# Batch 0's start in a fused linear attention and MLP kernel: k's sums as columns, k^T v in one stretch, chunk 0's denominators early

## The chip, the cores and the metric

The kernel runs on one core of a Trainium2 chip. A core has a matrix engine (TensorE, PE in the profile, with its weight loads listed as PEld), a vector engine (VectorE, DVE), an activation engine (ScalarE, ACT), a general engine (GpSimd, POOL) and a queue engine (SyncE, SP). Each runs its own stream of instructions in order; semaphores between them say when an operand is ready. PSUM is the memory that TensorE writes into, SBUF holds everything else. The metric is the device time of one execution in microseconds (us), lower is better.

## The reference

For 8 batches, 8 heads, 576 positions and head dimension 64 the reference computes a linear attention with cosine weights, and puts its output through a two-layer MLP:

```python
phi(x) = concat(relu(x) * cos_w, relu(x) * sin_w)     # 64 -> 128 features
kv  = einsum('bhsf,bhsd->bhfd', phi(k), v)            # k^T v, 128 x 64 per head
z   = sum_s phi(k)                                    # k's sums, 128 per head
num = einsum('bhsf,bhfd->bhsd', phi(q), kv)
den = einsum('bhsf,bhf->bhs', phi(q), z) + 1e-6
x   = (num / den), heads side by side                 # 4608 x 512
h   = x @ w_in                                        # 512 -> 2048
out = (h * sigmoid(1.702 * h)) @ w_out                # 2048 -> 512
```

## The kernel before

The two stages are fused batch by batch: the attention of a batch gives its x, transposed, and the MLP follows on it, while the attention of the next batch is slipped between the matmuls. The order on every engine is the order in which the program writes it (a manual schedule). Two kinds of PSUM tiles matter here: four "mm" tiles of one bank each, used in turn, and two "at" tiles of two banks each. A tile is written again only when the engine that reads it is done.

Batch 0 has nothing to be slipped between, so its attention is laid out by hand as a start, lines 386 to 436. Positions are cut in nine slices of 64 rows by 4 pairs of heads. The steps, by their helpers:

- `trig` (L142 on DVE and POOL, L140 on ACT) makes phi for one slice: two instructions, cosine and sine. k's nine slices (tile kr) come first, then q's (tile qn). k and q arrive in two transfers each from the SP queue, v for batch 0 in two transfers from POOL's queue straight into a bf16 tile vb (L132), one for heads 0 to 3 and one for heads 4 to 7. POOL's queue then brings the MLP's weights and batch 1's k, q and v.
- `idle(n)` (L348) issues n warm-up matmuls of 512 columns on a zero tile, whose result nobody reads. They keep TensorE at work; the first twelve run before any data is there.
- `ksum(j)` (L217) adds k slice j to k's sums: the weights are a 128x2 selector of the two heads of a pair, the moving operand is the slice with its 512 columns, and the result is a tile of 2 rows by 512. After the ninth slice DVE copies it to SBUF as bf16 (tile zr, L402), and `ksum_turn` (L223, L224) turns it with four small transposes and copies it into column 64 of the tile kvs.
- `qturn_pe(c)` (L171) transposes two slices of q into an mm tile, and `qevac(c)` copies them to qT, on DVE (L181) or ACT (L179). There are five turns; the last has one slice.
- `kv_mm` (L207) computes k^T v for two pairs of heads, 36 matmuls, and `kv_evac` (L212) copies the result on DVE into columns 0 to 63 of kvs. The two halves use the two at tiles.
- `num_mm(c)` (L232) multiplies chunk c of 128 positions of q with kvs for all 8 heads: 64 columns of numerators and, from column 64, the denominator. It needs an at tile. `num_div(c)` does three instructions on DVE: add 1e-6 (den, L240), reciprocal (inv, L242), multiply (xn, L244).
- `xturn_mm(c)` (L262) transposes xn into the free part of the same at tile, and `xturn_evac` (L269) copies it on ACT into x. Only then is the at tile free for the chunk after next.
- `start_block` (L357 on) runs chunks 0 to 4 between the first MLP matmuls: `mm1_part` (L285) for groups 0 to 3 in pieces of 128 columns, then the four gelus on ACT (L290), then group 4 (the fifth of sixteen, counted from zero) with 512 columns, `mm1(b, 4)`, and after it the transposes of chunk 4. Groups 0 to 3 hold all four mm tiles, so group 4 starts when the first gelu has read its own. `start_block` is called for batch 0 and, with its first turns already done, for batch 1.

The order of the start before, on TensorE: sums of slices 0, 1, 2, 3, 6, 4, 7, 5, a warm-up matmul, the sum of slice 8, a warm-up, q's turn 0, two warm-ups, turns 1 and 2, the turning of the sums, first half of k^T v, turn 3, second half of k^T v, turn 4, numerators of chunks 0 and 1, four warm-ups, then `start_block`.

Of the kernel before, what the change touches and what calls it, by code (L numbers as in the profile page):

```python
# [9 lines left out]
F32 = mybir.dt.float32  # L10
BF16 = mybir.dt.bfloat16
AF = mybir.ActivationFunctionType
MUL = mybir.AluOpType.mult
ADD = mybir.AluOpType.add
# [5 lines left out]
def kernel(  # L20
# [9 lines left out]
    nc = tc.nc  # L30
    B, H, S, D = q.shape
# [4 lines left out]
    NS = S // 64  # L36
    MT = 512
    NI = H // 2
# [6 lines left out]
    small = ctx.enter_context(tc.tile_pool(name="small", bufs=3))  # L45
    pmm = ctx.enter_context(tc.tile_pool(name="pmm", bufs=4, space=PSUM))
# [24 lines left out]
    ident = const.tile([128, 128], BF16)  # L71
# [13 lines left out]
    sel = const.tile([128, 2], BF16)  # L85
# [9 lines left out]
    kr = one.tile([128, NS, NI, 128], BF16, name="kr")  # L95
# [4 lines left out]
    qT = one.tile([128, H, 640], BF16, name="qT")  # L100
# [34 lines left out]
    def trig(dst, src, j, act=False, eng=nc.vector):  # L135
        i = src[:, :, ts(j, 64)]
        for cs, w in enumerate((cosw, sinw)):
            o = dst[:, j, :, ts(cs, 64)]
            if act:
                nc.scalar.activation(o, i, AF.Relu, scale=w[:, j:j + 1])  # L140
            else:
                eng.tensor_scalar(o, i, 0.0, w[:, j:j + 1], op0=MAX, op1=MUL)  # L142
# [24 lines left out]
    def qturn_pe(c, home=None):  # L167
        tp = pmm.tile([128, 2, NI, 128], BF16, name="mm") if home is None else home
        for j in range(2 * c, min(2 * c + 2, NS)):
            for i in range(NI):  # L170
                nc.tensor.transpose(tp[:, j % 2, i], qn0[:, j, i, :], ident)  # L171
        tps[c] = tp

    def qevac(c, act=False):
        n = min(2 * c + 2, NS) - 2 * c
        o = qT[:, :, ds(c * 128, n * 64)].rearrange("f h (j p) -> f j h p", j=n)
        i = tps.pop(c)[:, 0:n].rearrange("f j i (hh p) -> f j (i hh) p", hh=2)
        if act:
            nc.scalar.activation(o, i, AF.Copy)  # L179
        else:  # L180
            nc.vector.tensor_copy(o, i)  # L181
# [10 lines left out]
    st = {}  # L192

    def kv_open(i0=0, i1=NI):
        t = pat.tile([128, 2, 512], F32, name="at")
        for i in range(i0, i1):
            st["kv", i] = t[:, :, ds((i - i0) * 65, 65)]
        st["ps", i0] = t[:, :, 0:(i1 - i0) * 65]
        if i0 == 0:
            st["kvs"] = small.tile([128, 2, NI, VW], BF16, name="kvs", bufs=2)  # L200

    def kv_mm(i0, i1, rhs, col, n):
        for i in range(i0, i1):
            for j in range(NS):
                for hh in range(2):
                    r = slice(hh * 64, hh * 64 + 64)
                    nc.tensor.matmul(st["kv", i][:, hh, ds(col, n)], kr[r, j, i, :], rhs(r, i, j),  # L207
                                     start=(j == 0), stop=(j == NS - 1))

    def kv_evac(i0, i1, n=65):  # L210
        o = st["kvs"][:, :, i0:i1, 0:n]
        nc.vector.tensor_copy(o, st["ps", i0].rearrange("p hh (i e) -> p hh i e", e=65)[:, :, :, 0:n])  # L212

    def ksum(j):
        if j == 0:
            st["z"] = pmm.tile([128, 512], F32, name="mm")
        nc.tensor.matmul(st["z"][0:2], sel, kr[:, j].rearrange("p i f -> p (i f)"),  # L217
                         start=(j == 0), stop=(j == NS - 1))

    def ksum_turn():  # L220
        zt = pmm.tile([128, NI, 2], BF16, name="mm")
        for i in range(NI):
            nc.tensor.transpose(zt[:, i], st["zr"][:, ts(i, 128)], ident[0:2, 0:2])  # L223
        nc.vector.tensor_copy(st["kvs"][:, :, :, 64], zt.rearrange("f i hh -> f hh i"))  # L224

    nums = {}

    def num_mm(c):
        ps = pat.tile([128, 2, 512], F32, name="at")
        for h in range(H):  # L230
            i, hh = divmod(h, 2)
            nc.tensor.matmul(ps[:, h // 4, ds((h % 4) * 65, 65)], qT[:, h, ts(c, 128)],  # L232
                             st["kvs"][:, hh, i, 0:65], start=True, stop=True)
        nums[c] = [ps]

    def num_div(c):
        ps = nums[c][0]
        pv = ps[:, :, 0:260].rearrange("p a (h e) -> p a h e", h=4)
        den = small.tile([128, 2, 4], F32, name="den")
        nc.vector.tensor_scalar(den, pv[:, :, :, 64], 1e-6, None, op0=ADD)  # L240
        inv = small.tile([128, 2, 4], F32, name="inv")
        nc.vector.reciprocal(inv, den)  # L242
        xn = small.tile([128, 2, 4, 64], BF16, name="xn", bufs=4)
        nc.vector.tensor_tensor(xn, pv[:, :, :, 0:64],  # L244
                                inv.unsqueeze(3).to_broadcast([128, 2, 4, 64]), op=MUL)
        nums[c].append(xn)
# [7 lines left out]
    def x_open(b):  # L254
        x[b] = xpool.tile([128, KC, S], BF16, name="xT")

    def xturn_mm(c):
        ps, xn = nums[c]
        xv = xn.rearrange("p a h e -> p (a h e)")
        for kc in range(KC):  # L260
            o = ps[:, kc // 2, ds(264 + (kc % 2) * 64, 64)].bitcast(BF16)
            nc.tensor.transpose(o, xv[:, ts(kc, 128)], ident)  # L262

    def xturn_evac(b, c):
        ps = nums.pop(c)[0]
        n = 128 if c < 4 else 64
        i = ps[:, :, 264:392].bitcast(BF16).rearrange("p a (k t) -> p a k t", k=2)[:, :, :, 0:n]
        o = x[b][:, :, c * 128:c * 128 + n].rearrange("p (a k) t -> p a k t", a=2)
        nc.scalar.activation(o, i, AF.Copy)  # L269
# [11 lines left out]
    def mm1_part(b, fc, t0, t1):  # L281
        if t0 == 0:
            hp[fc] = pmm.tile([128, MT], F32, name="mm")
        for kc in range(KC):
            nc.tensor.matmul(hp[fc][:, t0:t1], w_in_of(kc, fc), x[b][:, kc, t0:t1],  # L285
                             start=(kc == 0), stop=(kc == KC - 1))

    def gelu(fc):
        g = gpool.tile([128, MT], BF16, name="g")
        nc.scalar.activation(g, hp.pop(fc), AF.Gelu_apprx_sigmoid)  # L290
        gT[fc] = g

    def mm1(b, fc):
        mm1_part(b, fc, 0, MT)
        gelu(fc)
# [48 lines left out]
    def idle(n, w=None):  # L344
        if w is None:
            w = pmm.tile([128, 512], F32, name="mm")
        for _ in range(n):
            nc.tensor.matmul(w, warm[:, 0:128], warm, start=True, stop=True)  # L348
        return w
# [7 lines left out]
    def start_block(b, opened=False):  # L357

        if not opened:
            xturn_mm(0)  # L360
            xturn_evac(b, 0)
            num_mm(2)
            num_div(2)
            xturn_mm(1)
            xturn_evac(b, 1)
        for c in range(4):
            for fc in range(4):
                mm1_part(b, fc, c * 128, c * 128 + 128)
            if c == 0:
                num_mm(3)  # L370
                num_div(3)
                xturn_mm(2)
                xturn_evac(b, 2)
            if c == 1:
                num_mm(4)
                num_div(4)
                xturn_mm(3)
                xturn_evac(b, 3)
        for fc in range(4):
            gelu(fc)  # L380
        mm1(b, 4)
        xturn_mm(4)
        xturn_evac(b, 4)


    w = idle(12)
# [5 lines left out]
        trig(kr, kf, j)  # L392
    kv_open(0, 2)
    kv_open(2, 4)
    for j in (0, 1, 2, 3, 6, 4, 7, 5):
        ksum(j)
    idle(1, w)
    ksum(8)
    for j in (0, 1):
        trig(qn0, qf0, j)  # L400
    st["zr"] = small.tile([2, 512], BF16, name="zr", bufs=1)
    nc.vector.tensor_copy(st["zr"], st["z"][0:2])  # L402
    idle(1, w)
    qturn_pe(0)
    for j in (2, 3):
# [10 lines left out]
    for j in (6, 7):  # L416
        trig(qn0, qf0, j, act=True)
    qevac(0)
    ksum_turn()
    qevac(2, act=True)  # L420
    kv_mm(0, 2, vb_rhs, 0, 64)
    qevac(1)
    kv_evac(0, 2, 64)
    qturn_pe(3)
    qevac(3, act=True)
    kv_mm(2, 4, vb_rhs, 0, 64)
    kv_evac(2, 4, 64)
    qturn_pe(4)
    qevac(4, act=True)
    num_mm(0)  # L430
    num_div(0)
    num_mm(1)
    num_div(1)
    idle(4)
    x_open(0)
    start_block(0)


# [61 lines left out]
    num_div(2)  # L500
    mm2(0, 3, 12, 16)
    start_block(1, opened=True)


# [78 lines left out]
```

## Time and profile before

| What | Value |
|---|---|
| Median of 3 runs | 294.69 us (294.63 to 295.33) |
| Profiled execution, its own time | 294.68 us |
| Span of the profile | 293.0 us |
| TensorE matmul busy | 287.1 us (98%) |
| TensorE weight load busy | 159.3 us (54%) |
| VectorE busy | 126.5 us (43%) |
| ScalarE busy | 131.1 us (45%) |
| GpSimd busy | 38.2 us (13%) |
| Granted TensorE clock, mean | 0.999 |

The span runs from the first to the last recorded instruction; the time of the execution has 1.7 us around it. Busy shares are averages over the whole run. The page's chain that ended last follows the work back from the last instruction, each step to what released it; by engine it is 95% PE. Matmuls are pipelined: one is listed with its latency, so the spacing of starts, not the listed duration, is what a row of them costs.

### The profile page before, as it was taken

What the parts mean: (1) busy time and instruction counts of PE and PEld (TensorE: products, weight loads), DVE (VectorE), ACT (ScalarE), POOL (GpSimd) and SP (SyncE); (2) the same over time, 40 slices, a digit from 0 to 9 for tenths busy, and PEclk for the clock granted to TensorE, in tenths of its full rate; (3) what the DMA queues carried; (4) which work ended last, traced back from release to release, by engine and by line L of the source; (5) the groups of instructions that cost most, each with busy time, mean ns of one, the idle gap of its engine ahead of it and who ended that gap; (6) DMA issues with size and microseconds to landing.
All of it is one profiled execution on the core that took longest, in us unless ns stands there. A gap on an engine that the chain in (4) does not pass through costs nothing.

```text
span 293.0 us, 5983 instructions
## 1 busy us (share of the span) xinstructions
PE 287.1 (98%) x2433; PEld 159.3 (54%) x2433; DVE 126.5 (43%) x364; ACT 131.1 (45%) x230; POOL 38.2 (13%) x70
## 2 busy tenths in 40 slices
PE   8989999999999999999999999999999999999995
PEld 2675656857455555455545554555455545565444
DVE  4864524692263826482558156715662420000000
ACT  7947752674114631463136412641265116773111
POOL 6760031500123001100110011001100010000000
PEclk9999999999999999999999999999999999999999
DMA  7999999585268965798469946986697440000322
GB/s 250 241 220 283 376 218 355 156 161 163 56 129 288 254 185 144 239 274 216 130 206 282 250 103 191 349 191 135 154 373 93 73 117 36 3 0 6 85 91 72
DMA packets 67227, 52.36 MB, mean 179 GB/s; under 512 B 47392, under 2 KB 57376, under 8 KB 67200
## 3 DMA queue, kind: packets, MB, share of 16 engines
q1 hardware_dynamic: 59824, 32.52, 45.1%
q0 software_dynamic: 7376, 19.47, 23.4%
q8 instruction: 19, 0.31, 0.4%
q14 instruction: 8, 0.07, 0.1%
HBM read 36.70 MB, written 9.44 MB: 157 GB/s over the span
## 4 chain that ended last, share of the span: by engine, by line
PE 95%; DMA 2%; DVE 1%; ACT 0%; issue 0%; SPq 0%; ACTq 0%
PE mm L335 43%; PE mm L285 38%; PE mm L303 4%; PE at L207 3%; PE at L232 3%; DMA kf<-in_k_dram 2%; PE mm L312 1%; PE at L262 1%; PE mm L171 1%; PE at L171 1%; DVE kr L142 1%; PE mm L217 0%; PE mm L348 0%; DVE xn L244 0%; ACT xT L269 0%
## 5 line engine op out<-in xcount | busy, mean ns | idle before, releaser
L335 PE MATMUL mm<-w_out_sb,g 128*128 128x512 bf16 (+1 forms) x528 | 117.7, 373 | 0.0
L285 PE MATMUL mm<-xT,w_in 128*128 128x512 bf16 (+1 forms) x608 | 113.5, 345 | 0.0
L290 ACT ACTIVATE g<-mm 128x512 bf16<-128x512 f32 x128 | 75.6, 598 | 32.0 <-PE mm L285 31.9
L285 PEld LDWEIGHTS <-w_in 128*128 128x128 bf16 x608 | 61.9, 114 | 49.0
L335 PEld LDWEIGHTS <-g 128*128 128x128 bf16 x528 | 48.7, 98 | 49.5
L339 ACT ACTIVATE ysb<-mm 128x512 f32<-128x512 f32 (+1 forms) x37 | 21.7, 586 | 111.4 <-PE mm L335 111.4
L342 POOL DMA_DIRECT2D out_dram<-ysb x38 | 20.6, 546 | 177.4 <-ACT ysb L339 177.2
L142 DVE TENSOR_SCALAR kr<-kf,cosw 128x256 bf16<-128x256 f32 x68 | 23.7, 349 | 29.0 <-DMA kf<-in_k_dram 29.0
L244 DVE TENSOR_TENSOR xn<-at,inv 128x512 bf16<-128x512 f32 x40 | 27.6, 691 | 1.4
L142 DVE TENSOR_SCALAR kr<-kf,sinw 128x256 bf16<-128x256 f32 x68 | 23.8, 350 | 0.0
L240 DVE TENSOR_SCALAR den<-at 128x8 f32<-128x8 f32 x40 | 6.6, 166 | 37.3 <-PE at L232 37.3
L232 PEld LDWEIGHTS <-qT 128*128 128x128 bf16 x320 | 14.6, 97 | 8.3 <-issue 1.0
L212 DVE CAST kvs<-at 128x520 bf16<-128x520 f32 (+1 forms) x9 | 5.8, 639 | 30.6 <-PE at L207 30.6
L232 PE MATMUL at<-kvs,qT 128*128 128x65 bf16 x320 | 16.1, 193 | 0.8 <-ACT xT L269 0.7
L155 DVE TENSOR_SCALAR qn<-qf,sinw 128x512 bf16<-128x512 f32 (+1 forms) x30 | 14.3, 477 | 0.0
L155 DVE TENSOR_SCALAR qn<-qf,cosw 128x512 bf16<-128x512 f32 (+1 forms) x30 | 14.3, 477 | 0.0
L303 PE MATMUL mm<-xt,w_in 128*128 128x384 bf16 x64 | 10.6, 326 | 0.0
L335 PE MATMUL mm<-w_out_sb,gl_t 128*128 128x512 bf16 x48 | 10.5, 379 | 0.0
L207 PEld LDWEIGHTS <-kr 64*128 64x128 bf16 x576 | 9.2, 94 | 2.3 <-issue 2.0
L303 PEld LDWEIGHTS <-w_in 128*128 128x128 bf16 x64 | 7.2, 113 | 3.3
L304 ACT ACTIVATE gl_t<-mm 128x384 bf16<-128x384 f32 x16 | 7.8, 490 | 2.4 <-PE mm L303 2.4
L163 DVE CAST vt<-vf 128x2304 bf16<-128x2304 f32 (+1 forms) x7 | 8.9, 1265 | 0.0
(68 smaller groups left out, 125.4 us busy)
## 6 DMA issues: line engine op xcount, KB each, us to landing
kf<-in_k_dram SPq DMA_DIRECT2D x5, 1152.0 KB, 6.7
vf<-in_v_dram SPq DMA_DIRECT2D x5, 1152.0 KB, 9.8
qf<-in_q_dram SPq DMA_DIRECT2D x5, 1024.0 KB, 6.0
out_dram<-ysb POOLq DMA_DIRECT2D x20, 256.0 KB, 2.8
kf<-in_k_dram POOLq DMA_DIRECT2D x2, 1152.0 KB, 10.3
vf<-in_v_dram POOLq DMA_DIRECT2D x2, 1152.0 KB, 14.0
out_dram<-ysb POOLq DMA_DIRECT2D x18, 128.0 KB, 2.9
w_in<-in_moe_w_in_dram POOLq DMA_DIRECT2D x4, 512.0 KB, 8.8
```

What stands on the lines that cost most here:

```text
L142: eng.tensor_scalar(o, i, 0.0, w[:, j:j + 1], op0=MAX, op1=MUL)
L155: nc.vector.tensor_scalar(o, i, 0.0, sc, op0=MAX, op1=MUL)
L163: nc.vector.tensor_copy(o, i)
L207: nc.tensor.matmul(st["kv", i][:, hh, ds(col, n)], kr[r, j, i, :], rhs(r, i, j), start=(j == 0), stop=(j == NS - 1))
L232: nc.tensor.matmul(ps[:, h // 4, ds((h % 4) * 65, 65)], qT[:, h, ts(c, 128)], st["kvs"][:, hh, i, 0:65], start=True, stop=True)
L244: nc.vector.tensor_tensor(xn, pv[:, :, :, 0:64], inv.unsqueeze(3).to_broadcast([128, 2, 4, 64]), op=MUL)
L285: nc.tensor.matmul(hp[fc][:, t0:t1], w_in_of(kc, fc), x[b][:, kc, t0:t1], start=(kc == 0), stop=(kc == KC - 1))
L290: nc.scalar.activation(g, hp.pop(fc), AF.Gelu_apprx_sigmoid)
L303: nc.tensor.matmul(hps, w_in_of(kc, fc), xt[:, kc, :], start=(kc == 0), stop=(kc == KC - 1))
L335: nc.tensor.matmul(yp[t, c0][:, c0:c1], w, w_out_sb[:, fc, c0:c1], start=(fc == 0), stop=(fc == FC - 1))
L339: nc.scalar.activation(ysb[:, c0:c1], yp[t, c0][:, c0:c1], AF.Identity)
L342: eng.dma_start(out=dst[:, c0:c1], in_=ysb[p0:p0 + n, c0:c1])
```

## The change

Seven edits in batch 0's start, and one in `start_block`, which batch 1 uses too:

1. `ksum(j)` takes the slice itself as weights, four times 128x128, and the selector's 2 columns as the moving operand. The sums then come out as columns, 128 rows by 4 pairs by 2 heads, in one bank: 36 matmuls of 2 columns in place of 9 of 512.
2. One copy on DVE (`ksum_evac`) brings them straight into column 64 of kvs, ahead of q's slices 4 and 5 on DVE. The tile zr, its copy and the four small transposes are gone.
3. One warm-up matmul goes ahead of each of the sums of slices 3, 6, 4, 7 and 5, five more than before.
4. `den_early(0)`: after the first half of k^T v, eight matmuls of one column (column 64 of kvs alone) give chunk 0's denominators in an mm tile; DVE adds 1e-6 and takes the reciprocal ahead of both copies of k^T v. `num_div(0)` then only multiplies.
5. The second half of k^T v and its copy move ahead of q's turn 3, the fourth turn.
6. The copy of q's turn 1 on DVE takes the place of the sums' copy, right behind that of turn 0.
7. q's turn 4 moves behind the numerators of chunks 0 and 1, its copy from ACT to DVE, behind `num_div(1)`; two warm-up matmuls follow instead of four.
8. In `start_block` the transposes of chunk 4 move ahead of `mm1(b, 4)`. Their copy on ACT stays where it was, behind group 4's gelu.

```diff
     def ksum(j):
         if j == 0:
-            st["z"] = pmm.tile([128, 512], F32, name="mm")
-        nc.tensor.matmul(st["z"][0:2], sel, kr[:, j].rearrange("p i f -> p (i f)"),
-                         start=(j == 0), stop=(j == NS - 1))
-
-    def ksum_turn():
-        zt = pmm.tile([128, NI, 2], BF16, name="mm")
+            st["z"] = pmm.tile([128, NI, 2], F32, name="mm")
         for i in range(NI):
-            nc.tensor.transpose(zt[:, i], st["zr"][:, ts(i, 128)], ident[0:2, 0:2])
-        nc.vector.tensor_copy(st["kvs"][:, :, :, 64], zt.rearrange("f i hh -> f hh i"))
+            nc.tensor.matmul(st["z"][:, i], kr[:, j, i, :], sel, start=(j == 0 and i == 0),
+                             stop=(j == NS - 1 and i == NI - 1))
+
+    def ksum_evac():
+        nc.vector.tensor_copy(st["kvs"][:, :, :, 64], st["z"].rearrange("f i hh -> f hh i"))
...
+    def inv_of(d):
+        den = small.tile([128, 2, 4], F32, name="den")
+        nc.vector.tensor_scalar(den, d, 1e-6, None, op0=ADD)
+        inv = small.tile([128, 2, 4], F32, name="inv")
+        nc.vector.reciprocal(inv, den)
+        return inv
+
+    def den_early(c):
+        d = pmm.tile([128, 2, 4], F32, name="mm")
+        for h in range(H):
+            nc.tensor.matmul(d[:, h // 4, h % 4:h % 4 + 1], qT[:, h, ts(c, 128)],
+                             st["kvs"][:, h % 2, h // 2, 64:65], start=True, stop=True)
+        return inv_of(d)
+
+    def num_div(c, inv=None):
         ps = nums[c][0]
         pv = ps[:, :, 0:260].rearrange("p a (h e) -> p a h e", h=4)
-        den = small.tile([128, 2, 4], F32, name="den")
-        nc.vector.tensor_scalar(den, pv[:, :, :, 64], 1e-6, None, op0=ADD)
-        inv = small.tile([128, 2, 4], F32, name="inv")
-        nc.vector.reciprocal(inv, den)
+        if inv is None:
+            inv = inv_of(pv[:, :, :, 64])
...
         for fc in range(4):
             gelu(fc)
+        xturn_mm(4)
         mm1(b, 4)
-        xturn_mm(4)
         xturn_evac(b, 4)
...
-    for j in (0, 1, 2, 3, 6, 4, 7, 5):
+    for j in (0, 1, 2):
+        ksum(j)
+    for j in (3, 6, 4, 7, 5):
+        idle(1, w)
         ksum(j)
     idle(1, w)
     ksum(8)
     for j in (0, 1):
         trig(qn0, qf0, j)
-    st["zr"] = small.tile([2, 512], BF16, name="zr", bufs=1)
-    nc.vector.tensor_copy(st["zr"], st["z"][0:2])
+    ksum_evac()
     idle(1, w)
     qturn_pe(0)
...
     qevac(0)
-    ksum_turn()
+    qevac(1)
     qevac(2, act=True)
     kv_mm(0, 2, vb_rhs, 0, 64)
-    qevac(1)
+    inv0 = den_early(0)
     kv_evac(0, 2, 64)
+    kv_mm(2, 4, vb_rhs, 0, 64)
+    kv_evac(2, 4, 64)
     qturn_pe(3)
     qevac(3, act=True)
-    kv_mm(2, 4, vb_rhs, 0, 64)
-    kv_evac(2, 4, 64)
-    qturn_pe(4)
-    qevac(4, act=True)
     num_mm(0)
-    num_div(0)
+    num_div(0, inv0)
     num_mm(1)
     num_div(1)
-    idle(4)
+    qturn_pe(4)
+    qevac(4)
+    idle(2)
     x_open(0)
     start_block(0)
```

More of the change, by code (lines that the diff above doesn't have):

```diff
@@ L234, in num_mm @@
         nums[c] = [ps]
-    def num_div(c):
+    def inv_of(d):
[11 more added lines that the diff above has]
+    def num_div(c, inv=None):
         ps = nums[c][0]
         pv = ps[:, :, 0:260].rearrange("p a (h e) -> p a h e", h=4)
-        den = small.tile([128, 2, 4], F32, name="den")
-        nc.vector.tensor_scalar(den, pv[:, :, :, 64], 1e-6, None, op0=ADD)
-        inv = small.tile([128, 2, 4], F32, name="inv")
-        nc.vector.reciprocal(inv, den)
+        if inv is None:
+            inv = inv_of(pv[:, :, :, 64])
         xn = small.tile([128, 2, 4, 64], BF16, name="xn", bufs=4)
```

## The prediction

> **What bounds the kernel now.** I read the busy time by stretches first, then the chain of work that ended last, then the timeline of the first 17 us. Of the stretches two rows matter (columns: busy time of PE, PEld, DVE, ACT and POOL with their instruction counts, then the granted clock, the DMA share and GB/s):
>
> ```profile
> 9.00:12.40 3.40, 3.40 (x70) 2.52 (x70) 3.28 (x10) 3.40 (x9) 2.57 (x2) 1.00 1.21 206
> ...
> 23.10:293.00 269.90, 266.51 (x2165) 146.27 (x2162) 112.05 (x318) 114.57 (x199) 23.76 (x42) 1.00 0.66 173
> ```
>
> From 23.1 us to the end PE is busy for 266.51 of 269.90 us at clock 1.00. Nothing that the change touches is there, apart from one order in batch 1, so an edit in batch 0's start is worth exactly as much as it brings forward the moment at which this dense stretch begins. That moment comes from the chain (start, length, what; a PE piece runs from the end of the instruction before it to the end of its own last one):
>
> ```profile
> 7.84 0.89 PE mm L217 x3
> ...
> 9.69 0.45 PE mm L171 x8
> 10.14 0.43 PE mm L348 x2
> 10.57 1.02 PE mm L171 x16
> 11.59 0.18 PE mm L223 x4
> 11.77 0.64 PE at L207 x36
> 12.41 0.55 PE mm L171 x8
> 12.96 0.66 PE at L207 x36
> ...
> 13.64 0.44 DVE kvs L212
> ...
> 14.12 0.29 PE at L232 x4
> ...
> 14.44 0.18 DVE den L240
> ...
> 14.64 0.21 DVE inv L242
> ...
> 14.87 0.70 DVE xn L244
> ...
> 15.62 0.41 PE at L262 x4
> ...
> 16.06 0.61 ACT xT L269
> ...
> 16.71 0.40 PE at L232 x8
> ...
> 18.22 0.24 PE at L232 x8
> ...
> 20.09 1.79 PE mm L285 x32
> ...
> 21.89 1.02 PE mm L285 x4
> 22.92 0.22 PE at L262 x4
> 23.14 9.50 PE mm L285 x44
> ...
> 39.95 0.89 PE at L171 x16
> ...
> 50.96 0.86 PE mm L335 x4
> ...
> 57.91 1.02 PE mm L285 x4
> ```
>
> The chain is TensorE alone from 7.84 to 13.6, then a relay: the copy of the second half of k^T v on DVE (13.64), chunk 0's numerators (14.12), its three divide steps on DVE (14.44, 14.64, 14.87), its transposes (15.62), their copy on ACT (16.06), and chunk 2's numerators (16.71), which need that copy to be done because it frees their PSUM tile. After them PE hardly waits. The transfers of batch 1 come early enough to leave the dense stretch alone: the latest that PE needs soon is q, whose first DVE use is the row below, while its transposes run only at the 39.95 piece above, some 6 us later.
>
> ```profile
> 33.73 0.35 DVE L142 TENSOR_SCALAR qn<-qf,cosw 128x256 bf16<-128x256 f32 x1 [2.83 <-DMA qf<-in_q_dram]
> ```
>
> **The change, step by step.** The timeline of before around the start (start, duration, engine, line):
>
> ```profile
> 1.25 4.91 PE L348 MATMUL mm<-warm 128*128 128x512 bf16 x12 [1.25 <-DVE warm L76]
> ...
> 8.29 0.49 ACT L140 ACTIVATE kr<-kf,sinw 128x256 bf16<-128x256 f32 x1
> ...
> 9.02 0.34 DVE L142 TENSOR_SCALAR qn<-qf,sinw 128x256 bf16<-128x256 f32 x1
> ...
> 9.40 0.68 DVE L402 CAST zr<-mm 2x512 bf16<-2x512 f32 x1
> ...
> 9.82 2.33 POOL L142 TENSOR_SCALAR qn<-qf,cosw 128x256 bf16<-128x256 f32 x1 [2.14 <-DMA qf<-in_q_dram]
> 9.88 0.49 ACT L140 ACTIVATE qn<-qf,sinw 128x256 bf16<-128x256 f32 x1
> ...
> 10.01 0.33 DVE L142 TENSOR_SCALAR qn<-qf,cosw 128x256 bf16<-128x256 f32 x1
> ...
> 10.80 0.34 DVE L142 TENSOR_SCALAR qn<-qf,sinw 128x256 bf16<-128x256 f32 x1
> 11.06 0.67 DVE L181 COPY qT<-mm 128x1024 bf16<-128x1024 bf16 x1
> ...
> 11.80 0.19 DVE L224 COPY kvs<-mm 128x8 bf16<-128x8 bf16 x1
> ...
> 12.15 1.13 POOL L142 TENSOR_SCALAR qn<-qf,sinw 128x256 bf16<-128x256 f32 x1
> ```
>
> The second half of v has these rows (two transfers, issued at 4.5 and 5.4):
>
> ```profile
> L132 POOL DMA_DIRECT2D vb<-in_v_dram x2: 756/835/914, 4.5 to 5.4; - x2
> ...
> DMA to landing us min/median/max: 6.2/6.5/6.8
> ```
>
> *k's sums.* Nine matmuls of 512 columns become 36 of two columns, each with its own load of 128x128 weights, and five more warm-up matmuls go between them. No row shows that form. The nearest is the four little transposes at 11.59: 0.18 for four, 0.045 each; the upper bound is a real transpose, 0.45 for eight (9.69), 0.056 each; the lower bound is a chunk's numerators, 0.24 for eight (18.22), 0.03 each with as large a load. So one k slice costs 0.18 (0.12 to 0.22), plus 0.22 for a warm-up matmul (0.43 for two, 10.14). I cost all of it at nothing up to the last slice: the slices wait for DVE and ACT, and the last one comes from ACT at 8.29 + 0.49 = 8.78. Then 0.18, a warm-up of 0.22, and q's first turn can start at about 9.2. It cannot finish before DVE's q slice 1 (9.02 + 0.34 = 9.36), four transposes and a latency of 0.2 later, so it ends near 9.8, against 10.14. If the slices cost double, this end stays, since DVE's slice covers 0.2 of it.
>
> *zr goes.* The sums were copied as 2x512 by DVE in 0.68 (9.40). The new copy is 128x8, as the one at 11.80: 0.19. It ends at about 9.5, and DVE's q slices 4 and 5 follow, 1.13 for the four (10.01 to 11.14). They also need q's second transfer, which had landed by 9.82, POOL's start on it. I take 9.7; bounds 9.5 (DVE free) and 9.82. They end at 10.83 (10.63 to 10.95) in place of 11.14.
>
> *q's turns.* Two warm-ups after 9.8 give 10.23; turn 1 needs ACT's slice 3 (9.88 + 0.49 = 10.37) and ends at 10.8; turn 2 needs the slices of 10.83, then four transposes and the latency, 0.44: it ends at 11.27, against 11.59. Four transposes of the sums (0.18) go.
>
> *k^T v and the early denominators.* The first half, 0.64, ends at 11.95. Then eight one-column matmuls for chunk 0's denominators: 0.36 at 0.045 each (0.24 to 0.45), done at 12.3. They need the first copy of qT, which on DVE moves up with the slices to about 10.75, plus 0.67: 11.42. The second half of k^T v would be next at 12.15, but it needs v's second transfer: 5.4 + 6.8 = 12.2. In before it had 0.7 us to spare there (12.96); now it is the gate. With 0.66 of work it ends near 12.95, against 13.62. So the denominators' matmuls are hidden behind v, up to 0.05.
>
> *DVE.* Denominator and reciprocal (0.18 and 0.21) are queued ahead of both copies of k^T v and wait for PE at 12.3: they end at 12.72. The two copies, 0.41 each, follow: 13.1 and, behind PE's 12.95 as well, 13.45. Before: 13.64 + 0.44 = 14.08. If the denominators came 0.3 late, the second copy would too: the new wait lies just beside the path. q's fourth turn (0.55) now runs under these copies.
>
> *Chunk 0.* Its last four numerators run from 13.5 to 13.8 (0.29; before 14.12 to 14.41). The multiply needs no denominator and no reciprocal between (0.18 + 0.21 and two handovers, 14.44 to 14.87 in the chain), so it runs from 13.82 to 14.52 instead of 14.87 to 15.57: 1.05 earlier. On PE stand meanwhile chunk 1's numerators (0.24), q's last turn (0.22; POOL's slice is done by 12.15 + 1.13 = 13.28) and two warm-ups instead of four (0.43), to about 14.5: a tie with the multiply. Transposes 0.41 and copy 0.61 with their handovers bring chunk 2's numerators to 15.63, against 16.71. **First term: 1.08 us.** q's last copy moves from ACT to DVE, behind chunk 1's multiply and ahead of chunk 2's denominators; that copy is half of 0.67, and DVE is idle there by this reckoning (multiply over at 15.5, next numerators not before 15.9), so it costs nothing; were DVE full, chunk 2 would be late by 0.35. POOL's and SP's queues keep their order and every DMA its place.
>
> *Last turns of x ahead of group 5.* After the last piece of 128-column matmuls (20.09 + 1.79 = 21.88) group 5's four matmuls take 1.02, where four of that size take 0.86 (50.96): 0.16 is a wait for the PSUM tile that ACT's first gelu frees. The transposes (0.22) then follow. Moved ahead, they fill the wait: 21.88 to 23.14, or 1.26, becomes 0.22 + 0.86 = 1.08. The same helper serves batch 1 (57.91, again 1.02). **Second term: 2 x 0.18 = 0.36 us.** Its lower end is nothing.
>
> Sum: 1.08 + 0.36 = 1.44. The profiled execution took 294.68 us (span 293.0, 1.7 around it), and the median of the runs shown is 294.69, so it stands for them: 294.68 - 1.44 = 293.24; I say **293.2**.
>
> **Rivals.**
> *The gate of v.* The path now runs through v's second transfer at 12.2 and the denominators in front of two DVE copies. Each microsecond that either is late comes off the first term. For it: one execution shows the landing and the margin is 0.05. Against it: no DMA is issued otherwise. With both late by 0.6, and the second term whole, the gain is 0.48 + 0.36 = 0.84: **293.8**; with the second term lost as well, 294.2.
>
> *The clock falls.* This one ends on the other side. At the start twelve 512-column matmuls take 4.91, 0.41 each, against 0.86 / 4 = 0.215 later: TensorE can run at half pace. If it falls back at about 9 us because two-column matmuls, transposes and waits fill the stretch before, some 4.4 us of PE work from there to 14.5 would double (28 transposes 1.6, warm-ups 1.1, k^T v 1.3, small ones 0.4); waits hide about 1.2 of it, so 3.2 is lost: 294.68 - 1.44 + 3.2 = **296.4**. It decides once more than 2.3 us is lost. Against it: the clock stood at 1.00 in 9.00:12.40, whose PE work by chain and code was hardly more than transposes, four long matmuls and half of k^T v, and the new order has six long matmuls between 6.4 and 9.2, where before had nine with two weight columns and one.
> The Trainium skill, page "TensorE: Matmul & The Clock Gate", section "Part 4: PE-mode transpose", says that transposes do not count as PE work for the clock gate in the way that matmuls do; by that rule the stretch from 9.2 to 11.3 is at risk and the time is the 296.4 just worked out. The trace bears it out little: before's stretch was as full of transposes and kept its clock.
>
> *The reorder does nothing for the end.* If ACT's gelu is later by what PE gains, the second term is nought: 293.6, still faster.
>
> **How the numbers follow.** What a measurement of this kernel can tell from no change is about 0.3%, 0.88 us. The forecast case, a gain of 1.0 to 1.9: 0.70, all faster. The gate of v: 0.18, of which 0.03 faster and 0.15 within 0.3%. The clock: 0.08, slower. Something that no row shows, such as PE order or DVE and POOL holding each other up: 0.04, of which 0.03 slower. Faster 0.73, within 0.3% 0.16, slower 0.11. The low end takes the lower bounds of the slices (0.2), and the second half's margins, another 0.2: 292.8. The high end takes the gate case to 294.4; the clock case is left out.
>
> **What the changed kernel's profile would show.** Right: q's first turn ends before 9.9, DVE's slices 4 and 5 start before 9.85, the second half of k^T v starts at 12.2 to 12.4 behind DMA, chunk 0's multiply starts near 13.8 and chunk 2's numerators near 15.6; no gap ahead of group 5 in either batch; the 512-column stretch starts about 1.26 early. Wrong: a granted clock under 1.00 between 9 and 15, slices at 0.1 per matmul, chunk 0's multiply after 14.3, or a wait of PE for DVE or DMA after 23 us that before did not have.

## The result and the profile after

The changed kernel takes 293.37 us (median of 6 runs, 293.05 to 293.73), against 294.69 before: a ratio of 0.9954, with an interval of 0.9944 to 0.9964. It is faster by 1.3 us. The profiled execution took 293.47 us with a span of 291.8, which is 1.21 less than the 294.68 of the profiled execution before.

The busy time by stretches, with the same columns as before (PE, PEld, DVE, ACT and POOL with counts, granted clock, DMA share, GB/s):

```profile
9.00:12.40 3.40, 3.19 (x74) 2.33 (x70) 3.15 (x9) 3.40 (x9) 2.55 (x4) 1.00 1.21 205
...
21.90:292.00 270.10, 266.56 (x2166) 146.38 (x2163) 112.21 (x318) 114.81 (x200) 23.83 (x42) 1.00 0.65 175
```

The granted clock is 1.00 in every stretch, and from 21.9 us to the end PE is busy for 266.56 of 270.10 us. Before, it was 266.51 of the 269.90 from 23.1 us. So it is as dense as before, and it begins earlier: the gain lies ahead of it. The chain of work that ended last (start, length, what):

```profile
2.39 7.26 DMA qf<-in_q_dram
...
9.68 1.52 DVE qn L142 x4
...
11.64 0.64 PE at L207 x36
12.28 0.28 PE mm L244 x8
12.56 0.64 PE at L207 x36
...
15.87 0.40 PE at L230 x8
...
19.28 1.79 PE mm L295 x32
21.07 0.22 PE at L272 x4
21.29 10.36 PE mm L295 x48
31.65 2.13 PE mm L322 x64
...
67.48 2.13 PE mm L322 x64
```

Chunk 2's numerators, the end of the relay, come at 15.87 instead of 16.71: 0.84 earlier. The transposes ahead of group 4 (the prediction's "group 5") stand at 21.07, directly behind the 128-column matmuls, and the 512-column matmuls follow them without a piece of 1.02 for four. Two pieces of the chain of before show what that adds:

```profile
32.64 2.13 PE mm L312 x64
...
68.65 2.13 PE mm L312 x64
```

At the first of them the changed kernel leads by 32.64 - 31.65 = 0.99, at the second, in batch 1, by 68.65 - 67.48 = 1.17. The timeline of the changed kernel around the start:

```profile
9.27 0.18 DVE L222 CAST kvs<-mm 128x8 bf16<-128x8 f32 x1
...
9.68 0.35 DVE L142 TENSOR_SCALAR qn<-qf,cosw 128x256 bf16<-128x256 f32 x1 [0.23 <-DMA qf<-in_q_dram]
9.84 1.20 POOL L142 TENSOR_SCALAR qn<-qf,cosw 128x256 bf16<-128x256 f32 x1 [2.18 <-DMA qf<-in_q_dram]
...
9.95 0.57 DVE L142 TENSOR_SCALAR qn<-qf,sinw 128x256 bf16<-128x256 f32 x1
...
10.43 0.34 DVE L142 TENSOR_SCALAR qn<-qf,cosw 128x256 bf16<-128x256 f32 x1
...
10.70 0.49 DVE L142 TENSOR_SCALAR qn<-qf,sinw 128x256 bf16<-128x256 f32 x1
...
12.49 0.71 PE L207 MATMUL at<-vb,kr 64*128 64x64 bf16 x36
...
12.92 0.75 DVE L212 CAST kvs<-at 128x256 bf16<-128x256 f32 x2
...
14.04 0.69 DVE L254 TENSOR_TENSOR xn<-at,inv 128x512 bf16<-128x512 f32 x1 [0.37 <-PE at L230]
```

The sums' copy is the 0.18 at 9.27. The two cosine instructions on DVE (9.68 and 10.43) take 0.35 and 0.34, but the two sine instructions (9.95 and 10.70) take 0.57 and 0.49, where before all four took 0.33 or 0.34. POOL's cosine instruction, which lies beside them, now takes 1.20 instead of 2.33, and it begins 0.16 after DVE's first one (9.84 against 9.68), where before it began 0.19 ahead of it (9.82 against 10.01).

### The profile page after: what moved, and what is told of

The parts are those of the page before. It is cut to its first block, busy times and chain, and to the rows that moved or that the text cites. A ratio compares the mean times of both kernels' runs of the same rounds, so it can differ in the third digit from the quotient of the medians.

```text
span 291.8 us, 6048 instructions
## 1 busy us (share of the span) xinstructions
PE 286.0 (98%) x2467; PEld 160.1 (55%) x2467; DVE 126.6 (43%) x364; ACT 130.4 (45%) x229; POOL 37.2 (13%) x70
## 4 chain that ended last, share of the span: by engine, by line
PE 95%; DMA 2%; DVE 1%; SPq 0%; ACT 0%; issue 0%; ACTq 0%
PE mm L345 43%; PE mm L295 38%; PE mm L313 4%; PE at L230 3%; PE at L207 3%; DMA qf<-in_q_dram 2%; PE mm L322 1%; PE at L272 1%; PE at L171 1%; DVE qn L142 1%; PE mm L171 0%; SPq L62 0%; ACT xT L279 0%; SPq L63 0%; PE mm L358 0%
## 5 line engine op out<-in xcount | busy, mean ns | idle before, releaser
L358 PE MATMUL mm<-warm 128*128 128x512 bf16 x23 | 8.6, 494 | 1.2 <-DVE warm L76 1.2
```

## The experiments

All of them are timed against the kernel before on the same chip. "Chunk 2's numerators" is their start in the experiment's own trace: 16.71 before, 15.87 in the changed kernel. Two runs of one kernel differ there as well, because q's second transfer does not land at the same moment each time (9.65 in the first run of the changed kernel, 9.50 in the second).

| kernel | median us | ratio to before (interval) | chunk 2's numerators |
|---|---|---|---|
| changed | 293.37 | 0.9954 (0.9944 to 0.9964) | 15.87 |
| changed, run again | 293.29 | 0.9949 (0.9937 to 0.9962) | 15.72 |
| start only | 293.61 | 0.9967 (0.9955 to 0.9979) | 16.43 |
| turns of x only | 294.37 | 0.9999 (0.9987 to 1.0011) | 16.76 |
| without early denominators | 293.59 | 0.9966 (0.9954 to 0.9979) | 15.98 |
| k^T v's second half behind q's fourth turn | 293.89 | 0.9977 (0.9967 to 0.9986) | 16.20 |
| without the five warm-ups | 294.33 | 0.9979 (0.9966 to 0.9992) | 16.93 |
| q's slice 8 on ACT | 293.40 | 0.9961 (0.9948 to 0.9974) | 15.60 |
| the same, its transfer behind v | 293.27 | 0.9949 (0.9937 to 0.9961) | 15.65 |
| sums as rows | 294.85 | 0.9999 (0.9990 to 1.0008) | 15.87 |
| sums as rows, padded | 293.88 | 0.9977 (0.9967 to 0.9987) | 15.95 |

**The changed kernel again**, as a yardstick for the others, with no edit:

> The changed kernel itself, beside the other kernels of this group on the same chip. Ratio to the kernel before 0.9945 to 0.9965; its profile as in the first one, DVE's two sine instructions of slices 4 and 5 at 0.5 or more, and q's turn 2 as late after the landing of q's second transfer as there (last transpose 11.42 at a landing of 9.65, 1.8 us).

It gave 293.29, 0.08 from the first run, and DVE's sine instructions took 0.57 and 0.49 again. From DVE's start on slice 4 (9.52) to the first half of k^T v (11.42) lie 1.90 us, against 1.89 in the first trace (9.68 to 11.57).

**The two terms apart.** One kernel is the changed one with edit 8 undone, the other is the kernel before with edit 8 alone. The edit of the second:

```diff
+        xturn_mm(4)
         mm1(b, 4)
-        xturn_mm(4)
```

> The changed kernel with the transposes of chunk 4 put back behind the 512-column matmuls: batch 0's start alone. Theory: the start is worth 0.8 to 0.95 us, so 0.36 slower than the changed kernel (ratio to before 0.9970). Rival (most of the gain was the reorder, or the two overlap): the start alone gives under 0.6 (ratio over 0.998) or all of it (0.9956).

> The kernel before with one edit: the transposes of chunk 4 ahead of group 5's... first 512-column matmuls, in both batches that use them. Theory: 0.18 twice, 0.36 us faster than before (ratio 0.9988). Rival (the first gelu frees its tile later by as much): ratio 1.000.

The start alone gives 0.9967, as expected. The turns alone give 0.9999, and the interval holds both the expected 0.9988 and no change: by time this one says nothing. Its trace does. The chain of waits and work of the kernel with the turns alone:

```profile
20.14 1.79 PE mm L285 x32
21.93 0.22 PE at L262 x4
...
32.51 2.12 PE mm L312 x64
...
57.76 0.22 PE at L262 x4
...
68.34 2.12 PE mm L312 x64
```

From the end of the 128-column matmuls (20.14 + 1.79 = 21.93) to the next kind of matmul, 32.51, lie 10.58 us; before, it was 32.64 - 21.88 = 10.76. That is 0.18, and again 0.18 in batch 1 (68.34 - 57.76 = 10.58 here, 68.65 - 57.89 = 10.76 before).

The profiled execution of the start alone shows something else. Its timeline, where DVE comes to q's slice 4:

```profile
10.23 0.35 DVE L142 TENSOR_SCALAR qn<-qf,cosw 128x256 bf16<-128x256 f32 x1 [0.64 <-DMA qf<-in_q_dram]
```

q's second transfer landed late, and the whole start ran 0.55 behind that of the changed kernel (9.68). This execution took 294.37, the other five of this kernel 293.38 to 293.65. Before, DVE was at the copy of zr and came to slice 4 only at 10.01, so a landing up to about then held up nothing on DVE. In the changed kernel the landing is on the path.

**What slowed DVE's slices.** The suspect is POOL, which works on q's slice 8 at the same time. In this experiment ACT does that slice, behind its copy of q's turn 2, and POOL computes no slice:

```diff
-    trig(qn0, qf0, 8, eng=nc.gpsimd)
...
     qevac(2, act=True)
+    trig(qn0, qf0, 8, act=True)
```

> The changed kernel with q's slice 8 made on ACT, behind the copy of q's turn 2, instead of on POOL beside DVE's slices 4 and 5. Theory (DVE and POOL hold each other up there): DVE's two sine instructions, 0.57 and 0.49 in the changed kernel, go back to about 0.33; slice 5 ends near 10.8 instead of 11.19, q's turn 2 and the first half of k^T v come 0.3 to 0.4 earlier, and the second half starts at 12.2, behind the landing of v at 12.14, instead of 12.49: chunk 2's numerators 0.25 earlier, some 0.25 us faster than the changed kernel (ratio to the kernel before about 0.9947 where the changed kernel has 0.9954). Rival (the sines are long for another reason, such as q's transfer landing): the sines stay at 0.5 to 0.57 and nothing moves.

The timeline of this kernel:

```profile
9.37 0.35 DVE L142 TENSOR_SCALAR qn<-qf,cosw 128x256 bf16<-128x256 f32 x1
...
9.64 0.35 DVE L142 TENSOR_SCALAR qn<-qf,sinw 128x256 bf16<-128x256 f32 x1
...
9.90 0.35 DVE L142 TENSOR_SCALAR qn<-qf,cosw 128x256 bf16<-128x256 f32 x1
...
10.17 0.35 DVE L142 TENSOR_SCALAR qn<-qf,sinw 128x256 bf16<-128x256 f32 x1
...
11.02 0.71 PE L207 MATMUL at<-vb,kr 64*128 64x64 bf16 x36
...
12.23 0.71 PE L207 MATMUL at<-vb,kr 64*128 64x64 bf16 x36 [0.22 <-DMA vb<-in_v_dram]
```

All four DVE instructions take 0.35 and end at 10.52, 1.15 after their start instead of 1.51. So POOL's work beside them is the cause of the slower slices. The first half of k^T v starts at 11.02 instead of 11.57, but not all of that is the edit: q's second transfer landed earlier in this execution, so that slice 4 began at 9.37 instead of 9.68. Counted from there the first half comes after 1.65 us instead of 1.89 or 1.90, a gain of about 0.25. The second half now does wait for v, which is the gate that the prediction had named, and starts at 12.23, 0.26 earlier than in the changed kernel's first trace and 0.12 earlier than in its second. The same 0.27 and 0.12 are left at chunk 2's numerators. The medians (293.40 against 293.37) show none of it; the expected 0.25 us of time did not come.

To move the gate, the next kernel also takes slice 8 of q out of q's second transfer and loads it behind v on POOL's queue:

```diff
-        nc.sync.dma_start(out=t[:, :, cut:S], in_=src_of(src, 0)[:, :, cut:S])
+        end = S if src is k else 512
+        nc.sync.dma_start(out=t[:, :, cut:end], in_=src_of(src, 0)[:, :, cut:end])
...
+    nc.gpsimd.dma_start(out=qf0[:, :, 512:S], in_=src_of(q, 0)[:, :, 512:S])
```

> As the kernel with q's slice 8 on ACT, and slice 8 also comes in a transfer of its own (128 KB) behind v on POOL's queue, so that q's second transfer is 512 instead of 640 KB and v has less ahead of it. Theory (the start now waits for q's second transfer, then for v's second half): both land 0.2 to 0.35 earlier, DVE's slice 4 starts at 9.45 or when they land, the second half of k^T v 0.2 to 0.3 earlier than 12.23, and the time is 0.2 to 0.3 us under the kernel with slice 8 on ACT, 0.4 under the changed one. Rival (the landings don't move, or slice 8 comes so late that turn 4 waits): same or slower.

q's second transfer landed at about 8.9 and v's at about 11.9, both earlier, as wanted. But the longer row of issues on POOL now lies beside DVE's slices of k (timeline of this kernel):

```profile
5.94 0.80 POOL L134 DMA_DIRECT2D qf<-in_q_dram  x1
...
6.18 0.68 DVE L144 TENSOR_SCALAR kr<-kf,cosw 128x256 bf16<-128x256 f32 x1 [0.61 <-DMA kf<-in_k_dram]
...
6.70 1.52 POOL L125 DMA_DIRECT2D w_in<-in_moe_w_in_dram  x2
...
7.04 0.56 DVE L144 TENSOR_SCALAR kr<-kf,cosw 128x256 bf16<-128x256 f32 x1
```

The three cosine instructions took 0.68, 0.56 and 0.56 and the sine instructions between them 0.33, so DVE came to q's slice 4 only at 9.64. The median, 293.27, is that of the changed kernel run again (293.29); the expected 0.4 under it did not come.

**The early denominators.** `den_early` goes, and `num_div(0)` works them out behind the numerators:

```diff
-    inv0 = den_early(0)
...
-    num_div(0, inv0)
+    num_div(0)
```

> The changed kernel without the early denominators: chunk 0 divides in three steps again. Theory, by the prediction's step: den and inv (0.18 and 0.21, with two handovers 0.43) go back between the numerators and the multiply, while the second half of k^T v, no longer behind eight small matmuls (0.28) and with v landed at 12.14, starts at 12.2 and its copy ends 0.25 earlier: net 0.15 to 0.2 slower than the changed kernel (ratio to before about 0.996). Rival (the early denominators cost nothing where they stand): the full 0.43 slower (ratio 0.997).

The timeline of this kernel:

```profile
12.37 0.98 DVE L212 CAST kvs<-at 128x256 bf16<-128x256 f32 x2
...
13.72 0.17 DVE L236 TENSOR_SCALAR den<-at 128x8 f32<-128x8 f32 x1 [0.37 <-PE at L230]
...
15.98 0.40 PE L230 MATMUL at<-kvs,qT 128*128 128x65 bf16 x8 [0.69 <-ACT xT L279]
```

The two copies of k^T v end earlier (12.37 + 0.98 = 13.35 against 12.92 + 0.75 = 13.67), but the denominator's two instructions stand ahead of the multiply, and chunk 2's numerators come 0.11 later than in the changed kernel's first trace and 0.26 later than in its second. Part of that is a later landing again: counted from DVE's start on slice 4 (9.72 here) they come after 6.26 us, against 6.19 and 6.20 in the two traces of the changed kernel. So by the traces the early denominators are worth less than 0.1, below the expected 0.15 to 0.2, and the rival's 0.43 does not occur. The medians lie 0.22 to 0.30 apart, too little to settle it with this spread of runs (293.35 to 294.59).

**The order of k^T v.** Its second half and its copy go back behind q's fourth turn, as before:

```diff
-    kv_mm(2, 4, vb_rhs, 0, 64)
-    kv_evac(2, 4, 64)
     qturn_pe(3)
     qevac(3, act=True)
+    kv_mm(2, 4, vb_rhs, 0, 64)
+    kv_evac(2, 4, 64)
```

> The changed kernel with the second half of k^T v put back behind q's turn 3; the early denominators and the rest stay. Theory (this order carries most of what the start gains): the second half starts near 13.05 instead of 12.4 to 12.5, its copy ends near 14.25 instead of 13.6, chunk 2's numerators near 16.4, and the time is 0.55 to 0.65 us over the changed kernel (ratio to before 0.997). Rival (the copies on DVE, behind the denominators, set the pace, so that the order of PE matters little): under 0.2 over it.

The timeline of this kernel:

```profile
12.82 0.71 PE L207 MATMUL at<-vb,kr 64*128 64x64 bf16 x36
...
13.57 0.42 DVE L212 CAST kvs<-at 128x256 bf16<-128x256 f32 x1 [0.42 <-PE at L207]
...
16.20 0.40 PE L230 MATMUL at<-kvs,qT 128*128 128x65 bf16 x8 [0.69 <-ACT xT L279]
```

The second half starts at 12.82 instead of 12.49, its copy runs from 13.57 instead of 13.24, and chunk 2's numerators come at 16.20, that is 0.33 later than in the changed kernel's first trace and 0.48 later than in its second. Counted from DVE's start on slice 4 (9.54 here) it is 6.66 us against 6.19 and 6.20: 0.46. The medians differ by 0.52 to 0.60. Of the edits of the start that were undone one at a time (this order, the early denominators, the sums as columns) it is worth most. The three together stay under the 0.84 of the start; edits 6 and 7 were not undone alone.

**The five warm-up matmuls.**

```diff
     for j in (3, 6, 4, 7, 5):
-        idle(1, w)
         ksum(j)
```

> The changed kernel without the five warm-up matmuls between k's sums. Theory (the clock doesn't hang on them, and the sums wait for DVE and ACT anyway): clock 1.00 from before 7 us on, the first turn of q at the same time or 0.05 earlier, time as the changed kernel within 0.15 us. Rival (the prediction's clock case): the clock falls to half, or comes up one stretch later, and TensorE's work from 9 to 14 us takes up to twice as long: 1 to 3 us slower.

The theory was wrong: they carry weight. The busy time by stretches of the changed kernel, ahead of 9.2 us:

```profile
5.60:9.20 3.60, 3.27 (x48) 1.92 (x47) 3.04 (x11) 2.94 (x8) 2.06 (x3) 1.00 1.10 365
```

and of the kernel without the five:

```profile
5.60:9.20 3.60, 2.35 (x43) 1.65 (x43) 3.04 (x10) 3.05 (x8) 1.89 (x3) 1.00 1.10 364
9.30:12.70 3.40, 3.40 (x32) 2.47 (x30) 2.95 (x8) 2.55 (x8) 2.96 (x4) 0.50 1.22 206
12.70:15.80 3.10, 3.04 (x109) 2.64 (x108) 1.74 (x6) 1.97 (x2) 3.10 (x6) 1.00 1.26 211
```

PE was busy for 2.35 us of the 3.60, against 3.27 (3.03 in the changed kernel's second trace), and the granted clock then fell to 0.50, for one stretch of 3.4 us. At what share it falls the runs do not tell. The timeline of PE in that stretch:

```profile
9.09 1.01 PE L171 MATMUL mm<-ident,qn 128*128 128x128 bf16 x8
9.89 1.06 PE L358 MATMUL mm<-warm 128*128 128x512 bf16 x2
10.75 1.91 PE L171 MATMUL mm<-ident,qn 128*128 128x128 bf16 x16
```

Eight transposes take 1.01 there (0.66 in the changed kernel) and two warm-up matmuls 1.06 (0.59). Chunk 2's numerators come 1.06 later, at 16.93. In nine of the twelve executions the mean granted clock was 0.994 or less and the time 293.96 us or more; in the other three it was 0.998 or 1.000, and the time 293.22 to 293.33, that of the changed kernel. So the five matmuls cost nothing and hold the clock.

The Trainium skill, page "TensorE: Matmul & The Clock Gate", section "Part 1: The HAM clock gate (the "warmup" mystery)", gives a window of about 3.4 us for the gate, and the trace agrees: the half clock lasted 3.4 us. The same page's "Part 4: PE-mode transpose" says that transposes do not count as work of PE for the gate in the same way. As far as one stretch can tell, the trace speaks against that: the rows of the half-clock stretch hold 24 transposes, two long matmuls and, at the end, a few matmuls of k^T v, and behind it the clock came back.

**The sums as columns.** Here k's sums are rows again, as before (nine matmuls of 512 columns, the copy to zr, four small transposes, no five warm-ups); all else is changed:

```diff
-        for i in range(NI):
-            nc.tensor.matmul(st["z"][:, i], kr[:, j, i, :], sel, start=(j == 0 and i == 0),
-                             stop=(j == NS - 1 and i == NI - 1))
+        nc.tensor.matmul(st["z"][0:2], sel, kr[:, j].rearrange("p i f -> p (i f)"),
+                         start=(j == 0), stop=(j == NS - 1))
...
-    ksum_evac()
+    st["zr"] = small.tile([2, 512], BF16, name="zr", bufs=1)
+    nc.vector.tensor_copy(st["zr"], st["z"][0:2])
...
     qevac(0)
+    ksum_turn()
     qevac(1)
```

> The changed kernel with k's sums as rows again (nine matmuls of 512 columns, the copy of 2x512, four small transposes, no five warm-ups); the rest stays changed. Theory (what DVE gains by the short copy it loses to POOL on slices 4 and 5): DVE's slices run from 10.0 to 11.15 at 0.33 each while POOL's first takes over 2 us, the second half of k^T v starts near 12.6, and the time is 0.1 to 0.25 us over the changed kernel. Rival (the prediction's step: 0.3 for turn 2 and 0.18 for the small transposes): 0.4 to 0.5 over it.

Its start is no later than the changed kernel's first trace and 0.15 later than its second (chunk 2's numerators at 15.87). Yet its median is 294.85, as slow as before. The time is lost at 70.8 us, in the chain of this kernel:

```profile
69.57 1.19 PE at L207 x72
70.76 1.62 issue
72.38 5.13 PE mm L347 x23
77.51 0.24 PE at L232 x8
```

Between the 72 small matmuls of batch 2's k^T v and matmuls of the MLP's second layer (L347) the chain has 1.62 us in which the trace names nothing that PE waits for. Some 0.16 of it is no loss: 24 of those matmuls run there and 23 are on record. Neither the kernel before nor the changed one has such a piece. The code there is the same in all of them; what differs is how many instructions PE has had before, and when it gets there. To test that, the next kernel adds 24 matmuls of two columns to `start_block`, in the part that only batch 0 runs, at a place where PE waits anyway. With their weight loads they are 48 instructions:

```diff
+            for _ in range(24):
+                nc.tensor.matmul(st["pad"][:, 0:2], warm[:, 0:128], warm[:, 0:2],
+                                 start=True, stop=True)
...
-    idle(2)
+    st["pad"] = idle(2)
```

> The kernel with the row sums (294.85) plus 24 two-column matmuls on the zero tile, results unread, in batch 0 behind the first turn of x, where TensorE waits 0.7 us for ACT. That kernel's start was only 0.15 us behind the changed one (512-column stretch from 21.10 against 20.95), but at 70.6 its TensorE stood still for 1.8 us with no semaphore to wait for, behind batch 2's 72 small matmuls of k^T v. Theory (the stall hangs on where TensorE's instruction stream is cut when it is brought in, and 48 instructions more move the cut): the stall at 70 is gone, the time falls by some 1.3 us to 293.3 to 293.6. Rival (the stall belongs to the sums' form, or to transfers at that time): it stays, 294.8.

The same place in the chain of the padded kernel:

```profile
70.00 1.19 PE at L207 x72
71.19 5.29 PE mm L347 x24
76.47 0.24 PE at L232 x8
```

The stand-still is gone: from the 72 matmuls to the next numerators lie 76.47 - 70.00 = 6.47 us instead of 77.51 - 69.57 = 7.94, so that 1.47 had been lost. The kernel is 1.0 us faster than without the padding (293.88, short of the expected 293.3 to 293.6), and its first 512-column matmuls start 0.42 later (21.52 against 21.10). So the stall does not belong to the row form of the sums, which both kernels have. But the padding moves every later instruction of PE both in the stream and, by 0.42 us, in time, and which of the two counts these runs cannot tell. That PE waits for its instructions there is a guess that no row shows.

None of these kernels is faster than the changed one by more than its two runs differ.

## Why the prediction was right, and where it was not

The time was forecast as 293.2 and came out as 293.37. The sum said a gain of 1.44 for the profiled execution, and there it is 1.21; the missing 0.23 is all in the first term.

**The second term held.** Edit 8 gives 0.18 in each batch, as worked out from 1.02 against 0.86.

**The first term was mis-sized: 0.84 instead of 1.08.** The step that failed is the one on q's slices 4 and 5 on DVE, "1.13 for the four", "They end at 10.83 (10.63 to 10.95)". They started at 9.68, as forecast, and ended at 11.19. The 1.13 came from an execution in which POOL had begun its instruction while DVE was copying out of PSUM; there POOL was the one that was stretched. With the copy gone DVE begins on q first, POOL 0.16 behind it, and DVE's sine instructions take 0.57 and 0.49, so that the four take 1.51. The kernel with slice 8 on ACT shows that POOL is the cause: there the four take 1.15. The prediction had "DVE and POOL holding each other up" only as a remainder of 0.04.

From there the delay runs through: turn 2 ends at 11.64 instead of 11.27, the eight one-column matmuls end at 12.56 instead of 12.3, and chunk 0's multiply starts at 14.04 instead of 13.82. Of the 0.37 at turn 2 some 0.13 was taken up on the way, most of it by the one-column matmuls, which took 0.28 where the prediction had 0.36. One sum of the prediction is off, without effect: two copies of 0.41 behind 12.72 end at 13.54 and not at 13.45, but the pair took only 0.75 from 12.92, to 13.67. The gate of v, which the prediction set at 12.2 and at which it wanted to see the second half start "behind DMA", was not the limit: PE came to it at 12.49, when v had landed. The rival on that gate is real, but only once the slices are quicker, as the kernel with slice 8 on ACT shows.

**k's sums were cheaper than costed, and it did not matter.** In the timeline of the changed kernel twelve of the two-column matmuls in a row (at 6.05) took 0.44 and four (at 7.06) took 0.25, so each further one costs 0.024 and a slice of four 0.10, below the range of 0.12 to 0.22; q's turn 0 started at 9.14 and was over before 9.9 all the same. By the kernels with sums as rows, the columns are worth no more than 0.15 at the start.

**The five warm-ups, costed at nothing, cost nothing, but the reason was incomplete.** The prediction saw that "the new order has six long matmuls between 6.4 and 9.2" and took the clock as safe. It is safe because of the five that the change adds. Without them the clock rival is what happens in most executions. Its price was far too high: 3.2 us by the prediction, about 1.1 by the run, since only the 3.4 us of one stretch run at half pace and not all the work up to 14.5.

**The early denominators and the order of k^T v.** Both work as described, but by the traces, counted from DVE's start on slice 4, the first is worth less than 0.1 and the second 0.46. The forecast that "the new wait lies just beside the path" fits: the first copy of k^T v is held by the denominators (12.92 against 12.37 without them), but the second, on which chunk 0 waits, starts at 13.24, when PE has just ended its half at 13.20.

**A dependence that the prediction did not price.** The path now begins at the landing of q's second transfer, as the chain's 7.26 us piece says. An execution in which it lands late gives part of the gain back, as the 294.37 of the start alone shows; the prediction noted the landing (9.82) as a bound only.

## What to carry to other kernels

A duration in a trace belongs to what ran beside it and to what had begun first: when an edit changes which of two engines starts first on the same data, the price of both can change, so keep a stretched row of the same instruction as a bound. Filler matmuls that cost nothing may still be what holds the clock, so before trimming them read how busy PE would be, stretch by stretch. When an edit speeds up the start of a path, look for the transfer that becomes its new first piece, and when a kernel loses time in a place that the edit did not touch, look in the chain for a stand-still there before blaming the edit.

## What the runs showed of the hardware

**DVE and POOL share something.** Both work from and to SBUF here, on f32 tiles of 128x256. Without the other at work on q, a DVE instruction takes 0.33 to 0.35 and a POOL one 1.13 or 1.14. Side by side two outcomes were seen, each several times: DVE keeps 0.33 and POOL takes 2.13 to 2.33 (before, with the turns alone and with sums as rows, where POOL begins during DVE's copy out of PSUM, up to 0.19 ahead of DVE's first instruction on q or together with it), or DVE takes 0.57 and 0.49 in its second and fourth instruction and POOL 1.20 (the changed kernel, where POOL begins 0.16 behind DVE). Whether the order of the two starts or the copy decides, no run separates. Beside issues of DMAs by POOL some of DVE's instructions are longer too, 0.56 and 0.68. The Trainium skill, page "SBUF — State Buffer", section "SBUF: two separate sides", says that DVE and GpSimd share a pair of ports as an exclusive lock, which one instruction holds for its whole length while the other blocks; for DVE it names instructions in a 2-port mode or with two SBUF inputs, and no row shows which mode these run in. That they collide agrees with the trace; the whole length does not, for within POOL's single 1.20 (9.84 to 11.04) a DVE instruction began at 10.43 and was done at 10.77 in the usual 0.34.

**PE lost about 1.5 us with nothing to wait for that the trace names**, between a burst of 72 small matmuls (k^T v of batch 2) and the long ones behind it, in the trace of one kernel. In the trace of the same kernel with 48 instructions added some 50 us ahead of it, it was gone; the cause is open.
